# Attention scores on half of the array for every tile from 9 on, with the gate, count and logit steps moved

## The chip, the cores and the metric

The kernel runs on one core of one Trainium2 chip. The metric is the device time of one execution in microseconds. TensorE is called PE in the profile (its weight loads PEld), VectorE DVE, ScalarE ACT, GpSimd POOL, and the engine that issues most DMAs SP.

## The reference, cut to what matters

```
# attention: B=4, H=8, S=768, D=40, one decaying state per head
m_new = max(f_t + m, i_t)
C = exp(f_t + m - m_new) * C + exp(i_t - m_new) * outer(v_t, k_t)      # n likewise, with k_t
y_t = sigmoid(o_t) * (C @ q_t) / max(|n . q_t|, 1)
# x = y as (3072, 320); 8 experts, one for each token
logits = (x / (|x| + 1e-6)) @ (emb / (|emb| + 1e-6)).T / tau
e = argmax(logits);  gate = softmax(logits)[e]
x = gate * (relu(x @ w1[e]) @ w2[e])                                   # F = 1024
# dense gated layer for all tokens
out = (sigmoid(x @ w_gate) * (x @ w_val)) @ w_out                      # F = 1536
```

## The kernel before, in words

The attention runs in chunks of 128 positions. There are 6 chunks and 4 batches, so 24 tiles; tile i is chunk i // 4 of batch i % 4. The order in which each engine gets its work is written out by hand. Each engine takes its instructions in that order and waits where an operand is not ready.

For a tile, `st_S` makes the scores of 8 heads on PE (16 passes into two banks of PSUM) and calls its argument `then`, which issues other work. DVE then applies the mask twice (L463 `am`, L465 `s_ps`), ACT rounds each half to f16 (L464, L466 `ah`), POOL and DVE take the rests (L467, L471 `al`). Between L467 and L471 it calls `last`. `st_V` scales v by the input gate on POOL (`vw`), `st_V2` splits it (`vh` on ACT, `vl` on POOL). `st_AV` multiplies scores by v and state by q into `o_ps`. `post_ops` divides (`den`, x on DVE) and multiplies by the output gate (POOL, and DVE for the last four tiles). `st_XT` turns x on PE and copies it (`xt` on ACT), `st_logit` makes the logits (`l_ps`) and copies them into `rs` on DVE (L583). `st_U` makes the new state (`u_ps`, bank 5), and its `add` folds it into `cc` on DVE (L517).

In the main loop (L784), step i runs `st_AV(i)`, `st_XT(i-1)`, `post_ops(i)`, some queued side operations, `st_U(i)`, `st_S(i+3)` with `add` and `st_logit(i-1)` inside it, and `st_V(i+2)`. `st_S` uses four PSUM banks in turn, so scores of tile i+2 need the DVE to be done with those of tile i. `tp_ps` gives banks 6 and 7 in turn to all transposes, logits and counts; `o_ps` is in bank 4.

The scores can be made in two ways. k and q of an even head lie in partitions 0 to 39, those of an odd head in 64 to 103, and the other rows are zero. In the full way, each matmul takes 128 rows. In the half way (`HALF`, L718) it takes only the 40 rows of its head, so matmuls of even and odd heads use different halves of the array. Before, `HALF` holds tiles 9, 11, 13, 15, 17 and 19; tile 0 is made so as well.

`side(n)` takes n operations from the queue `sideq`. At first these are the six DVE operations of `gate_ops(2 * L, S)`, which make the gates of chunks 2 to 5 on 32 partitions x 512. Their exponentials follow at i = 5 (`st_gexp`), and `st_gates2` turns them with 8 transposes on PE. Every fourth step, `st_rank` counts on PE which place each token takes in its expert's list, and puts eight DVE operations into the queue. The running count `run` is added up on POOL. `st_order` sorts the experts by count and `st_index` builds the lists of rows.

`warm` and `fill` issue 128x512 matmuls whose result is not read. After the loop (L1388 on) the last four tiles are woven with the first expert's matmuls (`step`, L980 to L998). The rest of the kernel, experts and dense layer, is matmuls for some 600 us.

Of the kernel before, what the change touches and what calls it, by code (L numbers as in the profile page):

```python
# [22 lines left out]
def kernel(  # L23
# [46 lines left out]
    def bank(j, name):  # L70
        return psum.tile([P, 512], F32, tag=f"b{j}", name=name)
# [27 lines left out]
    ones_f = const.tile([P, P], F32, name="ones_f")  # L99
    tri_bf = const.tile([P, P], BF16, name="tri_bf")  # L100
    eofs = const.tile([P, NE], F32, name="eofs")
    run = const.tile([P, NE], BF16, name="run")
    rs = const.tile([P, NTILE, NE + 1], F32, name="rs")
    raw, ssq = rs[:, :, 0:NE], rs[:, :, NE]
    rmax = const.tile([P, NTILE], F32, name="rmax")
# [23 lines left out]
    def constants():  # L129
        nc.gpsimd.memset(ones_bf, 1.0)  # L130
        nc.gpsimd.memset(ones_f, 1.0)
        nc.gpsimd.memset(zeros, 0.0)
        nc.gpsimd.affine_select(
            out=tri_bf, in_=ones_bf, pattern=[[1, P]], compare_op=ALU.is_ge,
            fill=0.0, base=-1, channel_multiplier=-1,
        )
        ramp(eofs, [[NT, NE]], 0, 0, "eofs_i")
        ramp(run, [[NT // P, NE]], 0, 0, "run_i")
        ramp(pcol, [[0, 1]], 1, 1, "pcol_i")
        ramp(tv, [[1, NTILE]], 0, 0, "tv_i")  # L140
        ramp(iota_e, [[1, NE]], 0, 0, "iota_ei")
        ramp(blk, [[NT // P, NE], [1, GT]], 0, 0, "blk_i")
        ramp(iota_p, [[1, P]], 0, 0, "iota_i")
        for k in range(NE):
            nc.gpsimd.memset(win[:, 0, k:k + 1], float(WIN[k]))
            nc.gpsimd.memset(win[:, 1, k:k + 1], float(WIN[k] // P))
# [166 lines left out]
            out=yi, in0=yi, scalar1=-1.0, scalar2=float(0x5F3759DF), op0=ALU.mult, op1=ALU.add  # L313
        )

    def norm_steps():
        g = nc.gpsimd
        two = lambda o, x, u, w, op0, op1: g.tensor_scalar(out=o, in0=x, scalar1=u, scalar2=w, op0=op0, op1=op1)
        for _ in range(3):
            two(en_t, en_y, en_sq, en_y, ALU.mult, ALU.mult)  # L320
            two(en_t, en_t, -0.5, 1.5, ALU.mult, ALU.add)
            g.tensor_tensor(out=en_y, in0=en_t, in1=en_y, op=ALU.mult)
        g.tensor_tensor(out=en_y, in0=en_y, in1=en_sq, op=ALU.mult)
        two(en_t, en_y, 1e-6, tb, ALU.add, ALU.mult)

    def norm_scale():
        nc.vector.reciprocal(en_r, en_t)
# [66 lines left out]

    def st_gates2(lo, hi):
        n = (hi - lo) * BH
        tp = bank(5, "tp_r") if lo > 1 else tp_ps("tp_r")
        for u, src in ((0, aexp), (1, rexp)):
            for c in range(lo, hi):
                o = 256 * u + (c - lo) * BH  # L400
                nc.tensor.transpose(tp[:, o:o + BH], src[:, c * L:(c + 1) * L], ident[0:BH, 0:BH])
        for u, dst, sc in ((0, w_all, SV), (1, ri_all, SQ * SV)):
            nc.vector.tensor_scalar_mul(
                dst[:, lo:hi].rearrange("p c s -> p (c s)"), tp[:, 256 * u:256 * u + n], sc
            )
# [169 lines left out]
    def st_logit(i):  # L575
        lp = tp_ps("l_ps")
        xt = xTt.pop(i)
        for kk in range(3):
            nc.tensor.matmul(
                lp[:, 0:NE], xt[:, kk * P:(kk + 1) * P], enT[:, kk, :],  # L580
                start=(kk == 0), stop=(kk == 2),
            )
        nc.vector.tensor_copy(raw[:, i, :], lp[:, 0:NE])  # L583

    def bc(t, n):
        return t.unsqueeze(2).to_broadcast([P, B, n])
# [6 lines left out]
    def st_rank(c):  # L593
# [4 lines left out]
        for b in range(B - 1):  # L598
# [1 line left out]
                rp[:, (b + 1) * NE:], ones_bf,  # L600
                sl[:, b:b + 1, :].to_broadcast([P, B - 1 - b, NE]), start=False, stop=False,
            )
        nc.tensor.matmul(
            rp, ones_bf, run.unsqueeze(1).to_broadcast([P, B, NE]), start=False, stop=True
        )
        for b in range(B):
            nc.gpsimd.tensor_tensor(out=run, in0=run, in1=sl[:, b, :], op=ALU.add)
        pf = bp.tile([P, B, NE], F32, tag="pf", name="pf", bufs=1)
        bm = bp.tile([P, 2, B], F32, tag="bm", name="bm")
        ob = bp.tile([P, B, NB], F32, tag="ob", name="ob")  # L610
# [18 lines left out]
                out=ob, in0=blk.unsqueeze(1).to_broadcast([P, B, NB]), in1=bc(bm[:, 0], NB), op=ALU.is_equal  # L629
            ),  # L630
            lambda: v.tensor_tensor(out=oh_b[:, cs, 0], in0=ob, in1=bc(tv[:, cs], NB), op=ALU.mult),
            lambda: v.tensor_scalar_mul(oh_b[:, cs, 1], ob, pcol),
        ]

    def st_order():

        v = nc.vector
        ps = tp_ps("ord_ps")
        nc.tensor.matmul(ps[:, 0:NE], ones_bf, run, start=True, stop=True)
        key = bp.tile([P, NE], F32, tag="key", name="key", bufs=1)  # L640
        m = bp.tile([P, NE, NE], F32, tag="om", name="om", bufs=1)
        r = bp.tile([P, NE], F32, tag="or", name="or_", bufs=1)
        a = lambda t: t.unsqueeze(1).to_broadcast([P, NE, NE])
        b = lambda t: t.unsqueeze(2).to_broadcast([P, NE, NE])
        return [
            lambda: v.tensor_tensor(out=key, in0=ps[:, 0:NE], in1=eofs, op=ALU.subtract),
            lambda: v.scalar_tensor_tensor(
                out=key, in0=key, scalar=float(NE), in1=iota_e, op0=ALU.mult, op1=ALU.subtract
            ),
            lambda: v.tensor_tensor(out=m, in0=a(key), in1=b(key), op=ALU.is_gt),  # L650
            lambda: v.tensor_reduce(out=r, in_=m, axis=AX.X, op=ALU.add),
            lambda: v.tensor_tensor(out=pick, in0=a(r), in1=b(iota_e), op=ALU.is_equal),
            lambda: v.tensor_tensor(out=m, in0=pick, in1=a(iota_e), op=ALU.mult),
            lambda: v.tensor_reduce(out=key, in_=m, axis=AX.X, op=ALU.add),
            lambda: v.tensor_copy(order, key),
        ]
# [58 lines left out]
                nc.gpsimd.indirect_dma_start(xrow[n][:, u], None, src, bass.IndirectOffsetOnAxis(at, 0))  # L715

    NAHEAD = 3
    HALF = range(9, NTILE - B + 1, 2)  # L718
    sideq = []

    def side(n=1):
# [20 lines left out]


    st_V(0)
    norm_steps()
    weave(gate_ops(L, 2 * L))
    st_V2(0)
    act_zero(qk[0])
    st_gexp(L, 2 * L)
    st_S(1, None, norm_scale)  # L750
    st_V(1)
    st_V(2)
    st_S(2, lambda: (st_AV(0), st_V2(1)), lambda: first_post(0))
    load(4)
    st_U(0)
    st_V2(2)
# [3 lines left out]
    st_sig(0)  # L760
    st_sig(1)
    post[0][5]()
    st_S(3, lambda: (st_AV(1), warm(2)), lambda: first_post(1))
    st_U(1)
    st_V2(3)
    post[1][5]()
    load(5)
    sideq += gate_ops(2 * L, S)
    side(1)
    turned = []  # L770
    st_S(
        4, lambda: (turned.extend(emb_T()), st_XT(0), st_AV(2), warm(2)),
# [1 line left out]
    )  # L774
    st_sig(2)
    load_kv(6)
    post[2][5]()
    side(1)
    st_V(4)
# [2 lines left out]
    side(1)  # L782
    GX = 4
    for i in range(3, NTILE - B):  # L784
        load(i + 4)
        if i > 3:
            st_AV(i)
            warm(2 if i < 8 else i > NTILE - B - 4)
            st_XT(i - 1)
            st_V2(i + 1)  # L790
            if i == GX + 1:
                st_gexp(2 * L, S)
            post = post_ops(i)
            if i == GX + 1:
                del post[3]
            weave(post)
        else:
            warm(3)
            st_logit(0)
            st_XT(2)  # L800
            st_V2(4)
        side(1 + (i > 16))
        if i == NTILE - B - 1:
            side(len(sideq))
# [4 lines left out]
        if i == NTILE - B - 2:  # L809
            od = st_order()  # L810
            od.pop(0)()
            sideq += od
        side(1 + (i > 16))
        if i > GX:
            side(1 + (i > 16))
        if i == NTILE - B - 1:
# [17 lines left out]
        if i > B and i % B == 1:  # L834
            rk = st_rank(i // B - 1)
            rk.pop(0)()
            sideq += rk
        if i == GX + 1:
            st_gates2(2, NCH)
        if i < NTILE - B - 1:  # L840
            st_V(i + 2)
        if i == GX:
# [328 lines left out]
    def offset_ops():  # L1171
# [4 lines left out]

        def counts():
            ps[0] = tp_ps("cnt_ps")
            nc.tensor.matmul(ps[0][:, 0:NE], ones_bf, run, start=True, stop=True)

        return [
            counts,
# [976 lines left out]
```

## Time and profile before

| | |
|---|---|
| time of three runs, median (lowest to highest) | 751.93 us (751.84 to 753.35) |
| time of the profiled execution | 752.99 us |
| its span, first to last instruction | 751.2 us |
| mean granted clock of TensorE | 0.993 |
| busy: PE, DVE, ACT, POOL | 728.3, 396.0, 375.5, 398.4 us |

Busy times are sums over the span. A matmul's end is modelled, so a busy PE is not PE at its peak. Times in the rows are counted from the first instruction.

### The profile page before, as it was taken

The numbers are of one execution on the slowest core, as the hardware profiler recorded it, in microseconds if no ns is written. First come the engines' busy times: TensorE is split into PE (matmuls) and PEld (weight loads), VectorE is DVE, ScalarE is ACT, GpSimd is POOL, SyncE is SP. The second block draws the span as 40 slices with busy tenths as digits, with TensorE's granted clock in tenths as the row PEclk, the third lists the DMA queues.
The fourth block names the chain that finished last, engine by engine and source line by source line (L and its number), as shares of the span: only waits on it lengthen the run. The fifth ranks groups of instructions, "written<-read, shape, count | busy, mean of one in ns | idle before, by whom it ended". The sixth has DMA issues, their size and how long they took to land. (4 is left out here: it accounts for less than half of the span.)

```text
span 751.2 us, 17720 instructions
## 1 busy us (share of the span) xinstructions
PE 728.3 (97%) x6910; PEld 650.1 (87%) x6910; DVE 396.0 (53%) x840; ACT 375.5 (50%) x863; POOL 398.4 (53%) x464
## 2 busy tenths in 40 slices
PE   6999999999999999999999999999999999999995
PEld 5889998898888989999788888888888888888884
DVE  7878888887678877865666574131121111111111
ACT  6777766456855656665455454323333333333322
POOL 8768887547766767886142324543334424424222
PEclk9999999899999999999999999999999999999998
DMA  7746775446445556651122220000000000000001
GB/s 232 214 133 188 252 220 158 130 133 187 124 141 166 153 164 191 182 155 46 54 78 61 81 67 15 28 36 2 1 11 28 1 2 36 1 2 37 1 1 40
DMA packets 39865, 70.47 MB, mean 94 GB/s; under 512 B 4818, under 2 KB 28460, under 8 KB 39772
## 3 DMA queue, kind: packets, MB, share of 16 engines
q1 hardware_dynamic: 36764, 59.61, 26.6%
q0 software_dynamic: 3008, 9.64, 3.9%
q8 instruction: 56, 0.92, 0.5%
q14 instruction: 37, 0.30, 0.1%
HBM read 60.55 MB, written 8.68 MB: 92 GB/s over the span
## 5 line engine op out<-in xcount | busy, mean ns | idle before, releaser
L1665 POOL TENSOR_TENSOR hl<-sgm,hh 128x512 fp32r<-128x512 f32 x71 | 94.8, 1340 | 226.2 <-ACT hh L1664 226.1
L1654 DVE TENSOR_TENSOR sgm<-v_ps,sgm 128x512 f32<-128x512 f32 (+1 forms) x73 | 49.7, 682 | 228.4 <-ACT sgm L1653 228.3
L1690 PE MATMUL o_ps<-wo,hl 64*128 64x320 f32 x560 | 87.7, 307 | 0.0
L1689 PE MATMUL o_ps<-wo,hh 64*128 64x320 f32 x560 | 87.2, 305 | 0.0
L1688 PE MATMUL o_ps<-wo,hh 64*128 64x320 f32 x560 | 86.7, 304 | 0.0
L1653 ACT ACTIVATE sgm<-g_ps 128x512 f32<-128x512 f32 (+1 forms) x73 | 43.2, 593 | 77.3 <-PE g_ps L1612 77.3
L1624 ACT COPY seen<-zeros 1x1 f32<-1x1 f32 x142 | 27.0, 190 | 108.1 <-PE v_ps L1612 60.8
L1664 ACT CAST hh<-sgm 128x512 fp32r<-128x512 f32 (+1 forms) x73 | 44.8, 615 | 46.5 <-DVE sgm L1654 46.2
L1072 ACT ACTIVATE hh<-h_ps 128x256 fp32r<-128x256 f32 (+7 forms) x72 | 35.2, 489 | 56.7 <-PE h_ps L984 55.9
L1688 PEld LDWEIGHTS o_ps<-wo,hh 64*128 64x128 f32 x560 | 53.4, 185 | 6.1
L1689 PEld LDWEIGHTS o_ps<-wo,hh 64*128 64x128 f32 x560 | 53.4, 184 | 5.6
L1610 PE MATMUL v_ps<-xg,wvh 64*128 64x512 f32 x144 | 56.4, 392 | 1.5 <-ACT seen L1624 1.5
L1611 PE MATMUL v_ps<-xl,wvh 64*128 64x512 f32 x144 | 56.4, 392 | 0.0
L1611 PE MATMUL g_ps<-xl,wgh 64*128 64x512 f32 x144 | 56.4, 392 | 0.0
L1611 PE MATMUL g_ps<-xg,wgh 64*128 64x512 f32 x144 | 56.4, 392 | 0.0
L1611 PE MATMUL v_ps<-xg,wvh 64*128 64x512 f32 x144 | 56.4, 392 | 0.0
L1610 PE MATMUL g_ps<-xg,wgh 64*128 64x512 f32 x144 | 56.4, 392 | 0.0
L1610 PE MATMUL g_ps<-xh,wgh 64*128 64x512 f32 x144 | 56.3, 391 | 0.0
L1610 PE MATMUL v_ps<-xh,wvh 64*128 64x512 f32 x144 | 56.3, 391 | 0.0
L1612 PE MATMUL g_ps<-xg,wgl 64*128 64x512 f32 x144 | 56.2, 390 | 0.0
L1612 PE MATMUL v_ps<-xh,wvl 64*128 64x512 f32 x144 | 56.2, 390 | 0.0
L1612 PE MATMUL v_ps<-xg,wvl 64*128 64x512 f32 x144 | 56.2, 390 | 0.0
(360 smaller groups left out, 2615.7 us busy)
## 6 DMA issues: line engine op xcount, KB each, us to landing
kv<-in_kvo_dram SPq DMA_DIRECT2D x24, 484.0 KB
w2raw<-in_moe_w_dram SPq DMA_DIRECT2D x32, 320.0 KB
w1raw<-in_moe_w_dram SPq DMA_DIRECT2D x32, 256.0 KB
qk<-in_qkt_dram SPq DMA_DIRECT2D x48, 160.0 KB
xs<-x SPq DMA_DIRECT2D x24, 192.0 KB
w1raw<-in_moe_w_dram SPq DMA_DIRECT2D x64, 64.0 KB
raw<-in_moe_w_out_dram SPq DMA_DIRECT2D x12, 320.0 KB
raw<-in_moe_w_gate_dram SPq DMA_DIRECT2D x8, 384.0 KB
```

The costliest lines, as they stand in the source:

```text
L1072: nc.scalar.activation(out=h[f][0], in_=ps, func=AF.Relu)
L1610: lambda: nc.tensor.matmul(ps, at(wh), h[rows, kk], start=start, stop=False),
L1611: lambda: nc.tensor.matmul(ps, at(wh), l[rows, kk], start=False, stop=False),
L1612: lambda: nc.tensor.matmul(ps, at(wl), h[rows, kk], start=False, stop=stop),
L1624: passed[key] = nc.scalar.copy(seen, zeros[0:1, 0:1])
L1653: nc.scalar.activation(out=s[:, cs], in_=pg[:, cs], func=AF.Sigmoid)
L1654: nc.vector.tensor_tensor(out=s[:, cs], in0=pv[:, cs], in1=s[:, cs], op=ALU.mult)
L1664: nc.scalar.copy(gh[:, cs], s[:, cs])
L1665: e.tensor_tensor(out=gl[:, cs], in0=s[:, cs], in1=gh[:, cs], op=ALU.subtract)
L1688: lambda: nc.tensor.matmul(o, gh[rows, ts_], wh[rows], start=begin, stop=False),
L1689: lambda: nc.tensor.matmul(o, gh[rows, ts_], wl[rows], start=False, stop=False),
L1690: lambda: nc.tensor.matmul(o, gl[rows, ts_], wh[rows], start=False, stop=end),
```

## The change

- `HALF` becomes every tile from 9 to 20, so tiles 10, 12, 14, 16, 18 and 20 are made the half way too. `warm` issues one matmul more at i = 9 and 13.
- The six gate operations are queued after `st_S(1)` instead of after `load(5)`, and one is taken per tile: inside `st_S(2)`, inside `st_S(3)`, after `post[2][5]`, after `st_S(5)`, at i = 3 and at i = 4. `st_gates2(2, NCH)` moves from the end of step 5 to step 6, after `st_AV(6)` and `st_XT(5)`, and uses a bank of `tp_ps` instead of bank 5.
- The norm of the expert embeddings: one of three Newton steps runs before `st_V2(0)` and the rest after it, and `norm_scale` moves from inside `st_S(1)` to inside `st_S(2)`.
- `run` keeps four counts, one for each place in the chunk. POOL adds a chunk in one operation instead of four, and PE sums the four with four small matmuls instead of one.
- The logits of tiles 19 to 23 are copied by ACT instead of DVE, and so is L632 (`oh_b[:, cs, 1]`), an ACT activation with a scale.
- `load_qk` runs one tile further ahead.

```diff
--- before.py
+++ after.py
@@ -99,7 +99,7 @@
     ones_f = const.tile([P, P], F32, name="ones_f")
     tri_bf = const.tile([P, P], BF16, name="tri_bf")
     eofs = const.tile([P, NE], F32, name="eofs")
-    run = const.tile([P, NE], BF16, name="run")
+    run = const.tile([P, 4, NE], BF16, name="run")
     rs = const.tile([P, NTILE, NE + 1], F32, name="rs")
     raw, ssq = rs[:, :, 0:NE], rs[:, :, NE]
     rmax = const.tile([P, NTILE], F32, name="rmax")
@@ -135,7 +135,8 @@
             fill=0.0, base=-1, channel_multiplier=-1,
         )
         ramp(eofs, [[NT, NE]], 0, 0, "eofs_i")
-        ramp(run, [[NT // P, NE]], 0, 0, "run_i")
+        nc.gpsimd.memset(run[:, 1:], 0.0)
+        ramp(run[:, 0], [[NT // P, NE]], 0, 0, "run_i")
         ramp(pcol, [[0, 1]], 1, 1, "pcol_i")
         ramp(tv, [[1, NTILE]], 0, 0, "tv_i")
         ramp(iota_e, [[1, NE]], 0, 0, "iota_ei")
@@ -313,15 +314,16 @@
             out=yi, in0=yi, scalar1=-1.0, scalar2=float(0x5F3759DF), op0=ALU.mult, op1=ALU.add
         )
 
-    def norm_steps():
+    def norm_steps(n, last=False):
         g = nc.gpsimd
         two = lambda o, x, u, w, op0, op1: g.tensor_scalar(out=o, in0=x, scalar1=u, scalar2=w, op0=op0, op1=op1)
-        for _ in range(3):
+        for _ in range(n):
             two(en_t, en_y, en_sq, en_y, ALU.mult, ALU.mult)
             two(en_t, en_t, -0.5, 1.5, ALU.mult, ALU.add)
             g.tensor_tensor(out=en_y, in0=en_t, in1=en_y, op=ALU.mult)
-        g.tensor_tensor(out=en_y, in0=en_y, in1=en_sq, op=ALU.mult)
-        two(en_t, en_y, 1e-6, tb, ALU.add, ALU.mult)
+        if last:
+            g.tensor_tensor(out=en_y, in0=en_y, in1=en_sq, op=ALU.mult)
+            two(en_t, en_y, 1e-6, tb, ALU.add, ALU.mult)
 
     def norm_scale():
         nc.vector.reciprocal(en_r, en_t)
@@ -394,7 +396,7 @@
 
     def st_gates2(lo, hi):
         n = (hi - lo) * BH
-        tp = bank(5, "tp_r") if lo > 1 else tp_ps("tp_r")
+        tp = tp_ps("tp_r")
         for u, src in ((0, aexp), (1, rexp)):
             for c in range(lo, hi):
                 o = 256 * u + (c - lo) * BH
@@ -580,7 +582,7 @@
                 lp[:, 0:NE], xt[:, kk * P:(kk + 1) * P], enT[:, kk, :],
                 start=(kk == 0), stop=(kk == 2),
             )
-        nc.vector.tensor_copy(raw[:, i, :], lp[:, 0:NE])
+        (nc.vector.tensor_copy if i < NTILE - B - 1 else nc.scalar.copy)(raw[:, i, :], lp[:, 0:NE])
 
     def bc(t, n):
         return t.unsqueeze(2).to_broadcast([P, B, n])
@@ -600,11 +602,11 @@
                 rp[:, (b + 1) * NE:], ones_bf,
                 sl[:, b:b + 1, :].to_broadcast([P, B - 1 - b, NE]), start=False, stop=False,
             )
-        nc.tensor.matmul(
-            rp, ones_bf, run.unsqueeze(1).to_broadcast([P, B, NE]), start=False, stop=True
-        )
         for b in range(B):
-            nc.gpsimd.tensor_tensor(out=run, in0=run, in1=sl[:, b, :], op=ALU.add)
+            nc.tensor.matmul(
+                rp, ones_bf, run[:, b:b + 1].to_broadcast([P, B, NE]), start=False, stop=(b == B - 1)
+            )
+        nc.gpsimd.tensor_tensor(out=run, in0=run, in1=sl, op=ALU.add)
         pf = bp.tile([P, B, NE], F32, tag="pf", name="pf", bufs=1)
         bm = bp.tile([P, 2, B], F32, tag="bm", name="bm")
         ob = bp.tile([P, B, NB], F32, tag="ob", name="ob")
@@ -629,14 +631,19 @@
                 out=ob, in0=blk.unsqueeze(1).to_broadcast([P, B, NB]), in1=bc(bm[:, 0], NB), op=ALU.is_equal
             ),
             lambda: v.tensor_tensor(out=oh_b[:, cs, 0], in0=ob, in1=bc(tv[:, cs], NB), op=ALU.mult),
-            lambda: v.tensor_scalar_mul(oh_b[:, cs, 1], ob, pcol),
+            lambda: nc.scalar.activation(out=oh_b[:, cs, 1], in_=ob, func=AF.Copy, scale=pcol),
         ]
+
+    def count(ps):
+
+        for b in range(B):
+            nc.tensor.matmul(ps, ones_bf, run[:, b], start=(b == 0), stop=(b == B - 1))
 
     def st_order():
 
         v = nc.vector
         ps = tp_ps("ord_ps")
-        nc.tensor.matmul(ps[:, 0:NE], ones_bf, run, start=True, stop=True)
+        count(ps[:, 0:NE])
         key = bp.tile([P, NE], F32, tag="key", name="key", bufs=1)
         m = bp.tile([P, NE, NE], F32, tag="om", name="om", bufs=1)
         r = bp.tile([P, NE], F32, tag="or", name="or_", bufs=1)
@@ -715,7 +722,7 @@
                 nc.gpsimd.indirect_dma_start(xrow[n][:, u], None, src, bass.IndirectOffsetOnAxis(at, 0))
 
     NAHEAD = 3
-    HALF = range(9, NTILE - B + 1, 2)
+    HALF = range(9, NTILE - B + 1)
     sideq = []
 
     def side(n=1):
@@ -742,15 +749,17 @@
 
 
     st_V(0)
-    norm_steps()
+    norm_steps(1)
     weave(gate_ops(L, 2 * L))
     st_V2(0)
+    norm_steps(2, True)
     act_zero(qk[0])
     st_gexp(L, 2 * L)
-    st_S(1, None, norm_scale)
+    st_S(1)
+    sideq += gate_ops(2 * L, S)
     st_V(1)
     st_V(2)
-    st_S(2, lambda: (st_AV(0), st_V2(1)), lambda: first_post(0))
+    st_S(2, lambda: (st_AV(0), st_V2(1)), lambda: (first_post(0), norm_scale(), side(1)))
     load(4)
     st_U(0)
     st_V2(2)
@@ -760,13 +769,11 @@
     st_sig(0)
     st_sig(1)
     post[0][5]()
-    st_S(3, lambda: (st_AV(1), warm(2)), lambda: first_post(1))
+    st_S(3, lambda: (st_AV(1), warm(2)), lambda: (first_post(1), side(1)))
     st_U(1)
     st_V2(3)
     post[1][5]()
     load(5)
-    sideq += gate_ops(2 * L, S)
-    side(1)
     turned = []
     st_S(
         4, lambda: (turned.extend(emb_T()), st_XT(0), st_AV(2), warm(2)),
@@ -774,6 +781,7 @@
     )
     st_sig(2)
     load_kv(6)
+    load_qk(7)
     post[2][5]()
     side(1)
     st_V(4)
@@ -782,10 +790,12 @@
     side(1)
     GX = 4
     for i in range(3, NTILE - B):
-        load(i + 4)
+        if i + 5 < NTILE:
+            load_qk(i + 5)
+        load_kv(i + 4)
         if i > 3:
             st_AV(i)
-            warm(2 if i < 8 else i > NTILE - B - 4)
+            warm(2 if i < 8 else i % B == 1 or i > NTILE - B - 4)
             st_XT(i - 1)
             st_V2(i + 1)
             if i == GX + 1:
@@ -799,6 +809,8 @@
             st_logit(0)
             st_XT(2)
             st_V2(4)
+        if i == GX + 2:
+            st_gates2(2, NCH)
         side(1 + (i > 16))
         if i == NTILE - B - 1:
             side(len(sideq))
@@ -810,7 +822,8 @@
             od = st_order()
             od.pop(0)()
             sideq += od
-        side(1 + (i > 16))
+        if i > GX:
+            side(1 + (i > 16))
         if i > GX:
             side(1 + (i > 16))
         if i == NTILE - B - 1:
@@ -835,8 +848,6 @@
             rk = st_rank(i // B - 1)
             rk.pop(0)()
             sideq += rk
-        if i == GX + 1:
-            st_gates2(2, NCH)
         if i < NTILE - B - 1:
             st_V(i + 2)
         if i == GX:
@@ -1176,7 +1187,7 @@
 
         def counts():
             ps[0] = tp_ps("cnt_ps")
-            nc.tensor.matmul(ps[0][:, 0:NE], ones_bf, run, start=True, stop=True)
+            count(ps[0][:, 0:NE])
 
         return [
             counts,
```

## Rows read from the trace of the kernel before

**Rows 1.** Busy time of each engine (instructions), granted clock, DMA, in stretches.

```profile
core 0: us, PE busy (x) PEld busy (x) DVE busy (x) ACT busy (x) POOL busy (x), PEclk, DMA share, GB/s
50.00:75.00 25.00, 24.93 (x392) 22.73 (x388) 21.10 (x61) 18.91 (x46) 18.52 (x31) 1.00 0.51 158
...
400.00:500.00 100.00, 100.00 (x1033) 88.37 (x1032) 47.74 (x102) 43.45 (x107) 34.78 (x28) 1.00 0.15 45
```

**Rows 2.** Waits of PE from 150 us on: total, times, longest.

```profile
PE v_ps L1610 <- ACT seen L1624: 1.5, 1, 1.5
PE tp_m L970 <- DVE xl L210: 0.5, 1, 0.5
```

**Rows 3.** The same stretches view, from one tile's scores to the next's.

```profile
44.11:51.65 7.54, 6.33 (x90) 5.81 (x88) 5.27 (x19) 5.26 (x11) 4.48 (x10) 1.00 0.71 242
...
56.52:61.59 5.07, 5.07 (x76) 4.85 (x74) 4.84 (x11) 3.32 (x9) 4.12 (x7) 1.00 0.75 240
61.59:65.96 4.37, 4.37 (x76) 4.03 (x74) 3.85 (x12) 3.11 (x9) 3.28 (x5) 1.00 0.34 107
```

**Rows 4.** Timeline of PE: scores and the work after; start us, length us.

```profile
51.65 1.16 PE L451 MATMUL s_ps<-qk 40*128 40x128 f32 x16
52.74 0.83 PE L579 MATMUL l_ps<-enT,xt 128*128 128x8 f32 x6
...
56.52 2.05 PE L451 MATMUL s_ps<-qk 128*128 128x128 f32 x16
58.41 0.73 PE L579 MATMUL l_ps<-enT,xt 128*128 128x8 f32 x6
...
104.73 2.05 PE L451 MATMUL s_ps<-qk 128*128 128x128 f32 x16
```

**Rows 5.** Timeline of PE where the gates of chunks 2 to 5 are turned.

```profile
48.07 0.40 PE L401 MATMUL tp_r<-ident,it 32*128 32x32 f32 x4 [1.21 <-DVE cc L517]
...
48.65 1.12 PE L480 MATMUL o_ps<-cst,qk 128*128 128x82 f32 x8
```

**Rows 6.** Waits of DVE and POOL from 52 to 123 us.

```profile
POOL vl L435 <- ACT vh L434: 10.6, 15, 1.9
...
DVE al L471 <- ACT ah L466: 4.3, 12, 0.4
...
DVE am L463 <- PE s_ps L451: 1.7, 2, 0.9
...
DVE am L463 <- POOL vl L435: 1.0, 1, 1.0
```

**Rows 7.** Timeline of DVE: the first mask of tiles 16, 20 and 22.

```profile
87.45 0.69 DVE L463 TENSOR_TENSOR am<-s_ps,cmask 128x512 f32<-128x512 f32 x1 [0.89 <-PE s_ps L451]
...
106.67 0.69 DVE L463 TENSOR_TENSOR am<-s_ps,cmask 128x512 f32<-128x512 f32 x1 [0.98 <-POOL vl L435]
...
121.67 0.69 DVE L463 TENSOR_TENSOR am<-s_ps,cmask 128x512 f32<-128x512 f32 x1
```

**Rows 8.** Groups of DVE from 56.52 to 104.73 us: busy us, mean ns.

```profile
L632 DVE TENSOR_SCALAR oh_b<-ob,pcol 128x128 bf16<-128x128 f32 x3 | 1.4, 477 | 0.0
```

**Rows 9.** The last four tiles: waits from 123 to 152 us.

```profile
PE l_ps L579 <- DVE rs L583: 1.1, 1, 1.1
...
DVE rs L583 <- PE l_ps L579: 1.0, 1, 1.0
...
PEld tp_x L567 <- DVE x L545: 0.4, 1, 0.4
```

**Rows 10.** The stretches view, last four tiles.

```profile
140.00:150.00 10.00, 8.72 (x49) 8.21 (x49) 8.44 (x24) 3.06 (x9) 5.28 (x9) 0.66 0.59 174
```

**Rows 11.** Waits from 14 to 24 us.

```profile
DVE al L471 <- ACT ah L466: 2.4, 2, 1.2
...
PE o_ps L488 <- POOL vl L435: 1.0, 1, 1.0
```

## The prediction, made before the changed kernel ran

> **What bounds the kernel now.** I read the stretches first. From 50 to 75 us PE is busy 24.93 of 25 us, and from 400 to 500 us all the time; the granted clock is 1.00 [rows 1]. After 150 us PE waits 2.0 us in all in its two largest waits, over 600 us [rows 2]. So what makes PE arrive earlier at 150 us makes the end earlier by the same, and the change is worth what it gives in the attention.
>
> There a busy PE says little, because VectorE is as full. I cut the loop at the scores of each tile. A step that holds a full tile took 5.07 us with DVE busy 4.84; the next, with a half tile, took 4.37 us with DVE busy 3.85 [rows 3]. DVE also waits in each tile for ACT's second rounding, 4.3 us in 12 times, 0.36 each [rows 6]; that wait lies inside a tile's own chain (mask, rounding, rest) and goes with no edit here. The pair then asks DVE for 4.84 + 3.85 + 2 x 0.36 = 9.41 us, and took 9.44. From 52 to 123 us DVE's other waits of note are for PE: 1.7 us in two, and 1.0 us in one that the view puts down to POOL [rows 6]. That last one is tile 20's mask at 106.67, whose full scores began at 104.73 [rows 4, 7]: 2.05 us of scores end just there, so it was PE too. So the loop is bound by DVE and PE in turns, with almost no slack between them.
>
> **Half-array scores.** From the start of the scores to the first logit matmul, a half tile holds PE for 52.74 - 51.65 = 1.09 us and a full one for 58.41 - 56.52 = 1.89 us [rows 4]. Six tiles change, so PE gets 6 x 0.80 = 4.8 us. If PE alone set the step this would be the gain, and it is the upper end. With DVE at 9.41 of 9.44 us a pair, a quicker PE helps only where DVE waited for PE's scores: 0.89 us at tile 16 and 0.98 at tile 20 [rows 7], both full tiles that become half ones. PE is 0.8 us quicker in that very tile, and already ahead from the tiles before, so I take 1.7 us of these 1.87. At the other changed tiles PE now waits instead, at `st_U`, whose bank is free only when DVE has done `cc`. The lower end is 0, if handing over between the engines eats it.
>
> The Trainium skill has a rule against this edit: in TensorEngine Tiling (Array Packing), under PSUM Bottleneck, it says that tiling speeds up the TensorE but not the emptying of PSUM, which may become the limit. The trace agrees, with DVE's 9.41 of 9.44 us [rows 3, 6]; by the rule this edit is worth about the 1.7 us, by PE's rows alone 4.8.
>
> **L632 to ACT.** Three of them took DVE 1.4 us, 477 ns each [rows 8]; a fourth lies between there and tile 22. One operation of DVE starts before the last has ended, so I count 1.4 us for all four (between 0.8 and 1.9). DVE is the bound in that stretch, so this is a gain. ACT was busy 3.32 and 3.11 us of the two steps [rows 3] and hides it.
>
> **Gate transposes.** At the end of step 5 they wait 1.21 us for bank 5, that is for DVE's `cc`, and hold up `st_AV(6)`, which starts at 48.65 [rows 5]. That step took 7.54 us with PE busy 6.33 [rows 3]. In step 6 they come behind `st_AV(6)` and `st_XT(5)`, with a bank of `tp_ps` emptied long before. The 8 transposes stay (48.65 - 48.07 = 0.58 us), the wait goes: 1.2 us, for PE and for DVE, which here waits for both. Lower end 0.6 if a bank of `tp_ps` is late; the upper is the 1.2. Their queue is DVE's: the two copies come before the masks of tile 9, whose scores are not there yet.
>
> **Gate operations, early.** Two of the six move to where DVE waited for ACT, 2.4 us in two times [rows 11]; that frees DVE between tiles 4 and 6. But PE has work without a gap there, with its `warm` matmuls, and POOL and ACT carry the chain before. I count 0. The norm: with eight of eleven POOL operations behind `vl(0)`, PE's wait of 1.0 us goes [rows 11], but `st_AV(1)` needs POOL's `vl(1)`, and POOL has the same work before it; 0 as well. `norm_scale` now lies on ACT between tile 2's roundings and the state copies, where ACT is busy; that can cost up to 0.6. For both together -0.6 to +1.0.
>
> **Counts, loads, warm.** POOL's four additions become one and PE gets three small matmuls per chunk. Two extra `warm` matmuls cost PE about 0.2 us each, in time that PE now has over. `load_qk` goes one tile earlier on SP, ahead of `load_kv`, past no wait that blocked it before. 0 together, hidden behind DVE's chain.
>
> **Last logits on ACT.** DVE stops waiting 1.0 us for `l_ps`, PE stops waiting 1.1 us for DVE's `rs`, and the 0.4 us for the last x shrinks, because DVE comes to it earlier [rows 9]. Behind that wait the clock was low: 140 to 150 us has a mean of 0.66, which is 10 x 0.34 = 3.4 us of PE work lost [rows 10]. PE can't get all this back, because the last ranks run through DVE, busy 8.44 of those 10 us. I take 2.0 us, DVE's wait of 1.0 and two copies with L632 for the rest. Lower end 0.4 (only the wait for x), upper 4.0 (with most of the clock's loss).
>
> **Sum.** Loop 1.7 + 1.4 + 1.2 = 4.3, less 0.5 for engines that now meet with no slack (an estimate from the 0.03 us that a pair had over, between 0 and 1.7), is 3.8; with the last tiles 5.8 us. The profiled execution took 752.99, its span 751.2; less 5.8 is 747.2. The runs' median is 1.06 lower, 751.93, so I expect **746.1 us**.
>
> **Rivals.**
> - *PE was the bound.* Then six halves give 4.8, less 0.4 for the `warm` matmuls, the gates 1.2 and the tail 4.0: 9.6 us, 742.3. PE busy in the pair for all 9.44 us speaks for it [rows 3], DVE's sum against. Chance 0.12.
> - *POOL or ACT takes DVE's place in the loop.* POOL waits for ACT's `vh` 10.6 us in 15 times [rows 6], and `vh` waits for POOL's `vw`; with its 4.12 us busy in a full step [rows 3], it can hold a step at 4.5 us or more. Then the loop keeps only the gates' 1.2 us, with up to 1.5 in the tail: 749.2. Chance 0.11.
> - *Nothing measurable.* The early part loses 0.6, the gates gain 1.2 and the tail 0.4: 750.9. Chance 0.07.
> - *The clock falls in the loop: slower.* More tiles with 40-row matmuls, and a PE that waits for DVE at each, can drop it. One spell like that of 140 to 150 us costs 3.4 us [rows 10]; two eat the gain (752.9), from three on the kernel is slower, 756.3. Against it: the clock was 1.00 all through 50 to 75 us, with every other tile half [rows 1], and the fall at 143 us came behind a PE wait of 1.1 us [rows 9]; the new waits are shorter. Chance 0.14. The Trainium skill, TensorE: Matmul & The Clock Gate, under What's actually happening, says that the clock follows how busy the array has been; the spell behind the wait agrees [rows 9, 10], and by it the time would be this rival's only if the loop's waits add up.
>
> **How the numbers follow.** The forecast has 0.56. Its own range is 743.5 to 748.5, from the ends of its terms that can come together. Faster by over 0.2% (1.5 us, about what a measurement here can tell) is the forecast, the first two rivals: 0.79. Within 0.2%: 0.07. Slower: 0.14. For 8 in 10 I go from 742.5, just above the first rival's point, to 750.0, which takes in the second; the slower case, no change and a little below stay out.
>
> **What would show it.** The profile after should have the half scores in tiles 9 to 20, no wait of 1.2 us before the gate transposes and tile 9's scores about 1.2 us earlier, at 50.4. DVE's mask of tile 22, at 121.67 before [rows 7], should start at about 117.9, with PE now waiting for `cc` in `st_U`. At 150 us the shift should be near 5.8, and stay to the end. I am wrong if the clock leaves 1.00 between 50 and 125 us, if the tail's shift is smaller than the loop's, or if steps of 4.6 us and more remain with DVE waiting for POOL or ACT.

## The result, and the profile after

The changed kernel took 742.49 us in the median (742.2 to 742.75), the kernel before 751.93: a ratio of 0.987, 95% interval 0.9853 to 0.9887. The profiled execution took 742.64 us with a span of 740.6 (752.99 and 751.2 before), so the span lost 10.6 us where the prediction's sum has 5.8. The medians are 9.44 apart: the profiled execution of the kernel before was 1.06 us slower than its median, that of the changed kernel 0.15. The time is 3.6 us below the forecast of 746.1 and just under the low end of the range. The mean clock of the profiled execution rose from 0.993 to 0.997.

Where the 10.6 us came up, by five places that both traces have:

| place | before | after | shift | predicted |
|---|---|---|---|---|
| scores of tile 8 start | 44.11 | 43.56 | 0.55 | 0 |
| scores of tile 9 start | 51.65 | 49.96 | 1.69 | 1.2 |
| first mask of tile 22 | 121.67 | 114.96 | 6.71 | 3.8 |
| first copy `seen` in the dense layer | 364.0 | 355.6 | 8.4 | 5.8 |
| last copy `seen` | 736.3 | 725.7 | 10.6 | 5.8 |

The stretches view of the changed kernel, with the columns of [rows 1]: the two long stretches, the step of tile 8, two steps of the loop, and the last tiles.

```profile
50.00:75.00 25.00, 24.95 (x404) 22.83 (x404) 22.28 (x65) 20.09 (x49) 20.07 (x29) 1.00 0.60 175
400.00:500.00 100.00, 100.00 (x1036) 87.07 (x1034) 45.29 (x94) 41.56 (x102) 38.31 (x31) 1.00 0.15 46
43.56:49.96 6.40, 6.32 (x94) 5.83 (x92) 4.73 (x16) 5.98 (x14) 3.91 (x6) 1.00 0.69 233
54.72:59.10 4.38, 4.33 (x75) 4.00 (x73) 4.25 (x10) 3.00 (x8) 3.25 (x5) 1.00 0.70 215
59.10:63.40 4.30, 4.30 (x73) 3.89 (x70) 3.76 (x12) 3.98 (x12) 3.50 (x6) 1.00 0.42 144
...
140.00:150.00 10.00, 9.37 (x82) 9.06 (x80) 9.21 (x29) 5.63 (x12) 4.00 (x4) 1.00 0.52 151
```

The step that holds the gate transposes went from 7.54 to 6.40 us with the same 6.32 of PE work: the wait is gone. The pair of steps that took 5.07 and 4.37 us [rows 3] takes 4.38 and 4.30, with DVE at 4.25 + 3.76. The clock of 140 to 150 us is 1.00 (0.66 before [rows 10]); a second profile of the changed kernel, f1 below, has a spell of low clock there.

The timeline of PE in the changed kernel: the transposes, and the scores of tiles 9 and 20.

```profile
48.22 0.49 PE L569 MATMUL tp_x<-ident,x 128*128 128x128 f32 x3
48.78 0.40 PE L403 MATMUL tp_r<-ident,it 32*128 32x32 f32 x4
49.03 0.41 PE L403 MATMUL tp_r<-ident,ft 32*128 32x32 f32 x4
49.37 0.66 PE L503 MATMUL u_ps<-vw,kv 128*64 128x41 f32 x16
49.96 1.16 PE L453 MATMUL s_ps<-qk 40*128 40x128 f32 x16
...
99.73 1.16 PE L453 MATMUL s_ps<-qk 40*128 40x128 f32 x16
```

The transposes follow `st_XT(5)` without the wait of 1.21 us [rows 5]. Tile 20 has half scores and starts 5.0 us earlier than in [rows 4]. DVE's first masks of tiles 16, 20 and 22, which waited 0.89, 0.98 and 0 us before [rows 7], now wait for nothing:

```profile
82.96 0.68 DVE L465 TENSOR_TENSOR am<-s_ps,cmask 128x512 f32<-128x512 f32 x1
...
101.01 0.68 DVE L465 TENSOR_TENSOR am<-s_ps,cmask 128x512 f32<-128x512 f32 x1
...
114.96 0.68 DVE L465 TENSOR_TENSOR am<-s_ps,cmask 128x512 f32<-128x512 f32 x1
```

The waits from 51 to 118 us and, from "PE r_ps" on, from 122 to 160 us (total, times, longest):

```profile
DVE al L473 <- ACT ah L468: 4.3, 12, 0.4
DVE am L465 <- PE s_ps L453: 0.4, 2, 0.2
...
PE r_ps L599 <- DVE sel L593: 1.8, 1, 1.8
PE tp_m L981 <- DMA xrow<-xs,idx: 0.6, 1, 0.6
```

DVE's wait for ACT inside a tile is what it was [rows 6], its waits for PE fell to 0.4 us, and the wait of PE in the last tiles has another releaser (a `sel` of the last rank) and grew from 1.1 [rows 9] to 1.8 us.

### The profile page after: what moved, and what is told of

It reads as the page before. It is cut to its first block, busy times and chain, and to the rows that moved or that the text cites. A ratio compares the mean times of both kernels' runs of the same rounds, so it can differ in the third digit from the quotient of the medians.

```text
span 740.6 us, 17763 instructions
## 1 busy us (share of the span) xinstructions
PE 719.4 (97%) x6936; PEld 650.8 (88%) x6936; DVE 393.3 (53%) x829; ACT 377.7 (51%) x874; POOL 395.9 (53%) x447
## 5 line engine op out<-in xcount | busy, mean ns | idle before, releaser
L1700 PE MATMUL o_ps<-wo,hh 64*128 64x320 f32 x560 | 89.0, 304 | 0.0
L1699 PE MATMUL o_ps<-wo,hh 64*128 64x320 f32 x560 | 88.9, 304 | 0.0
L1700 PEld LDWEIGHTS o_ps<-wo,hh 64*128 64x128 f32 x560 | 55.3, 184 | 5.3
L1699 PEld LDWEIGHTS o_ps<-wo,hh 64*128 64x128 f32 x560 | 55.3, 184 | 4.1
L1084 DVE SCALAR_TENSOR_TENSOR hl<-h_ps,hh 128x256 fp32r<-128x256 f32 (+7 forms) x72 | 39.5, 550 | 32.0 <-ACT hh L1083 31.6
L1621 PE MATMUL g_ps<-xg,wgh 64*128 64x512 f32 x144 | 56.4, 392 | 0.0
L1623 PE MATMUL g_ps<-xh,wgl 64*128 64x512 f32 x144 | 56.3, 391 | 0.0
```

The costliest lines, as they stand in the source:

```text
L1084: nc.vector.scalar_tensor_tensor(out=h[f][1], in0=ps, scalar=0.0, in1=h[f][0], op0=ALU.max, op1=ALU.subtract)
L1621: lambda: nc.tensor.matmul(ps, at(wh), h[rows, kk], start=start, stop=False),
L1623: lambda: nc.tensor.matmul(ps, at(wl), h[rows, kk], start=False, stop=stop),
L1699: lambda: nc.tensor.matmul(o, gh[rows, ts_], wh[rows], start=begin, stop=False),
L1700: lambda: nc.tensor.matmul(o, gh[rows, ts_], wl[rows], start=False, stop=False),
```

## The experiments

Each ratio is to the kernel before on the same chip in the same session. "Loop" is the time from the first mask of tile 10 to that of tile 22 in the profiled run, "dense" that between the first and last `seen`, and the last column is where, between 20 and 126 us, the granted clock fell from 1.00 to about 0.50 (1.2 GHz), called a spell below. Loop, dense and spells come from one profile of each run. In the cuts of the edits `...` stands for lines left out.

| run | ratio [95%] | loop | dense | clock low at |
|---|---|---|---|---|
| before (first chip) | | 62.76 | 372.3 | |
| changed (first chip) | 0.987 [0.9853, 0.9887] | 58.31 | 370.1 | |
| e1_half_only | 0.9999 [0.9977, 1.0021] | 62.81 | 373.3 | 49-53, 79-84 |
| e2_ohb_only | 0.9988 [0.9968, 1.0008] | 61.60 | 373.4 | 49-53 |
| e3_gates_only | 0.9959 [0.9944, 0.9974] | 63.27 | 373.3 | |
| e4_logits_only | 0.9994 [0.9979, 1.0009] | 62.75 | 373.3 | 50-55 |
| f1_after_again | 0.9873 [0.9857, 0.989] | 58.87 | 371.8 | 51-55 |
| f2_less_half | 0.9927 [0.991, 0.9943] | 62.37 | 371.7 | |
| f3_one_count | 0.9924 [0.9908, 0.9941] | 60.32 | 373.6 | |
| f4_ohb_on_vector | 0.9894 [0.9878, 0.9911] | 60.37 | 371.7 | |
| g1_run_size | 0.9976 [0.9959, 0.9993] | 62.70 | 371.3 | 48-55 |
| g2_pe_more | 0.992 [0.9898, 0.9941] | 61.89 | 371.3 | |
| g3_dve_more | 1.0004 [0.9981, 1.0026] | 68.82 | 371.3 | 77-88, 104-108 |
| g4_loop_trio | 0.9916 [0.9897, 0.9935] | 58.37 | 371.4 | 48-55 |
| h1_one_count_64 | 0.9915 [0.9885, 0.9944] | 60.40 | 371.3 | |
| h2_half_ohb_64 | 0.9935 [0.9919, 0.9952] | 61.71 | 371.4 | 48-52, 79-83 |
| h3_count_only | 0.9994 [0.9981, 1.0007] | 63.32 | 370.6 | 48-56 |
| h4_half_more | 0.9909 [0.9874, 0.9943] | 61.43 | 371.3 | 51-65 |
| p1_run_32 | 1.0001 [0.9981, 1.0021] | 62.70 | 372.3 | 49-54 |
| p2_run_80 | 1.0018 [0.9998, 1.0038] | 63.18 | 373.0 | 36-40, 50-54 |

**One part alone, in the kernel before.** e1_half_only takes the new half scores with their `warm` matmuls:

```diff
-    HALF = range(9, NTILE - B + 1, 2)
+    HALF = range(9, NTILE - B + 1)
...
-            warm(2 if i < 8 else i > NTILE - B - 4)
+            warm(2 if i < 8 else i % B == 1 or i > NTILE - B - 4)
```

> The kernel before, with only the half scores for tiles 9 to 20 and the two extra warm matmuls. Theory V (VectorE sets the step, as predicted): only the two waits of its mask for PE's scores go (0.89 and 0.98 us), so about 1.7 us faster, near 750.2. Theory P (PE sets the step): six halves of 0.80 less 0.4 for the warm matmuls, 4.4 us faster, near 747.5. The granted clock stays 1.00 from 50 to 125 us by both.

No gain shows. The interval leaves out Theory P's 4.4 us and just reaches Theory V's 1.7. Against both theories a spell came in the middle of the loop and took a part: outside it, the loop is shorter by 0.1 us from the mask of tile 10 to that of tile 14 (19.32 against 19.45) and by 0.4 from tile 16 to 22 (33.85 against 34.22).

e2_ohb_only moves L632 to ACT:

```diff
-            lambda: v.tensor_scalar_mul(oh_b[:, cs, 1], ob, pcol),
+            lambda: nc.scalar.activation(out=oh_b[:, cs, 1], in_=ob, func=AF.Copy, scale=pcol),
```

> The kernel before, with only the product with pcol (L632) on ScalarE. Theory V: VectorE loses four operations of its chain, 1.2 to 1.4 us faster, near 750.6. Theory P: no change, 751.9.

The loop is 1.16 us shorter, near the 1.4 of its term; the time's interval includes no change.

e3_gates_only has the gate operations one per tile and the transposes in step 6, without the edits to the norm:

```diff
-        tp = bank(5, "tp_r") if lo > 1 else tp_ps("tp_r")
+        tp = tp_ps("tp_r")
...
+    sideq += gate_ops(2 * L, S)
...
+        if i == GX + 2:
+            st_gates2(2, NCH)
...
-        if i == GX + 1:
-            st_gates2(2, NCH)
```

> The kernel before, with only the early gate operations one per tile and the eight transposes moved to step 6. Predicted 1.2 us faster (750.7), the wait of 1.21 us for bank 5 gone. If the early operations count as well, tile 9's scores start 1.7 us earlier as in the changed kernel (49.96 against 51.65), near 750.2.

It is the only part that is faster by itself by more than its interval. It is also the only one of the four with no low clock near 50 us. All nine of these kernels that keep the transposes at their old place, behind PE's wait of 1.1 to 1.2 us, have such a spell there; the profile of before hasn't. So e3's 2.5 us (751.68 against 754.20 in the medians) may hold the loss of a spell besides the 1.2 us.

e4_logits_only:

```diff
-        nc.vector.tensor_copy(raw[:, i, :], lp[:, 0:NE])
+        (nc.vector.tensor_copy if i < NTILE - B - 1 else nc.scalar.copy)(raw[:, i, :], lp[:, 0:NE])
```

> The kernel before, with only the last five logit copies on ScalarE. Predicted 2.0 us faster (749.9). If the low clock from 143 to 149 us came from PE's wait for VectorE's copy, it goes and up to 3.4 us come back (748.5); if the last ranks on VectorE hold all, 0.4 to 1 us.

The 2.0 us forecast did not come; the interval, from 1.6 us of gain to 0.7 of loss, leaves it out. PE's wait for `rs` is gone and the clock stays at 1.00 in the last tiles, but PE now waits there for two other operations of DVE (118 to 157 us):

```profile
PE r_ps L597 <- DVE sel L591: 1.9, 1, 1.9
PE ix_ps L663 <- DVE oh_b L632: 1.4, 1, 1.4
```

The four ratios multiply to 0.994, less than half of the change: something is missing, or the parts need each other.

**One part taken out of the changed kernel.** f1_after_again is the changed kernel on the chip of the three that follow.

> The changed kernel unaltered, as a base for the other three on the same chip. First mask of tile 10 to that of tile 22: 58.3 us as in its first profile (62.8 before). Granted clock 1.00 from 20 to 150 us.

The ratio is that of the first chip and the loop is 58.87 us, but the clock did not stay at 1.00: it fell at 51 us and again at 140 us, behind the wait of 1.8 us for `sel` that the first profile has too.

f2_less_half takes the two edits of e1 out again.

```diff
-    HALF = range(9, NTILE - B + 1)
+    HALF = range(9, NTILE - B + 1, 2)
...
```

> The changed kernel with the half scores of tiles 9, 11, ..., 19 alone and without the two extra warm matmuls. Theory V (VectorE sets the step): the two waits for PE's scores come back, 1.7 us slower than the changed kernel, 60.0 us from mask 10 to mask 22. Theory B (both bound: PE's time is worth its price once VectorE has been relieved): 3 to 4.4 us slower, 61.5 or more.

The half scores, which showed no gain alone, are worth 4.0 us here (749.82 less 745.84), as Theory B has it.

f3_one_count has a single running count again:

```diff
-    run = const.tile([P, 4, NE], BF16, name="run")
+    run = const.tile([P, NE], BF16, name="run")
...
-        nc.gpsimd.tensor_tensor(out=run, in0=run, in1=sl, op=ALU.add)
+        for b in range(B):
+            nc.gpsimd.tensor_tensor(out=run, in0=run, in1=sl[:, b, :], op=ALU.add)
```

> The changed kernel with one running count, added up by GpSimd in four operations, as before. Theory G (GpSimd's chain from the rest to the next v is what held VectorE's small operations): 1 to 2 us slower, most of it in the steps with ranks (masks 9 to 10, 13 to 14, 17 to 18). Theory V: within 0.3 us.

The part that the prediction priced at nothing costs 3.7 us when it is taken out: some 1.5 in the loop and 1.8 in the dense layer, where it does no work.

f4_ohb_on_vector takes out the edit of e2:

```diff
-            lambda: nc.scalar.activation(out=oh_b[:, cs, 1], in_=ob, func=AF.Copy, scale=pcol),
+            lambda: v.tensor_scalar_mul(oh_b[:, cs, 1], ob, pcol),
```

> The changed kernel with the product with pcol (L632) back on VectorE. Theory V: 1.2 us slower from mask 10 to 22, and the last ranks later by 0.3. If the shorter small operations of VectorE came with this edit (0.43 to 0.19 us each), 2 us and more slower.

1.7 us (747.56 less 745.84), near its term of 1.4.

**The dense layer: place or work?** g1_run_size, in the kernel before, only makes the tile of the count larger; no instruction differs but in addresses.

```diff
-    run = const.tile([P, NE], BF16, name="run")
+    run4 = const.tile([P, 4, NE], BF16, name="run")
+    run = run4[:, 0]
```

> The kernel before, in which only the tile of the running count is four times as large (64 instead of 16 bytes in each partition, three quarters unused), so that tiles behind it lie 48 bytes further. Theory A (the dense layer's pace depends on where its operands lie): from the first to the last reading of the dense layer's results on ScalarE 371.7 us instead of 373.3, and 1.7 us faster in all. Theory N (chance): no change, within 0.5 us.

The kernel is 1.8 us faster (752.45 against 754.21), and the dense layer 1 to 2 us quicker. Its first and last copy, in g1 and then in the kernel before:

```profile
L1625 ACT COPY seen<-zeros x142: 174/190/193, 364.4 to 735.7; 1x1 f32<-1x1 f32 x142
```

```profile
L1624 ACT COPY seen<-zeros x142: 186/190/193, 364.0 to 736.3; 1x1 f32<-1x1 f32 x142
```

735.7 - 364.4 = 371.3 us against 372.3 in this profile and 373.3 in e1 to e4. Two more sizes, which put everything behind the tile 16 and 64 bytes further instead of 48 (p1_run_32, shown, and p2_run_80 with 5 in place of 2):

```diff
-    run = const.tile([P, NE], BF16, name="run")
+    run4 = const.tile([P, 2, NE], BF16, name="run")
+    run = run4[:, 0]
```

> The kernel before with the tile of counts at 32 bytes per partition instead of 16, so that everything behind it lies 16 bytes further. Theory A (the place within 64 bytes decides, and the 48 bytes of the change end on a good one): the dense layer between its first and last copy takes 372.3 to 373.4 us as before, or a value between. Theory B (any place but the old one is quicker): 371.3 us and ratio 0.998, as with 48 bytes.

> The same with 80 bytes, so that everything lies 64 bytes further. Theory A (the place within 64 bytes decides): as before, 372.3 to 373.4 us and ratio 1.000. Theory B (any other place): 371.3 us and 0.998.

372.3 and 373.0: no gain. Every kernel with 48 bytes took 370.1 to 371.8, every other 372.3 to 373.6, on one chip too (f1, f2 and f4 371.7 to 371.8, f3 373.6). So the place decides, and 48 bytes is a better one than 0, 16 or 64. It shows in the matmuls themselves, of which this is one group of many, from 370 to 720 us (busy us, mean ns): the kernel before, then g1.

```profile
L1690 PE MATMUL o_ps<-wo,hl 64*128 64x320 f32 x530 | 83.1, 307 | 0.0
```

```profile
L1691 PE MATMUL o_ps<-wo,hl 64*128 64x320 f32 x532 | 81.8, 302 | 0.0
```

**Which engine bounds the changed loop?** g2_pe_more gives PE two `warm` matmuls more in each step from 8 to 19, g3_dve_more gives DVE a copy of 128x128 there.

```diff
-            warm(2 if i < 8 else i % B == 1 or i > NTILE - B - 4)
+            warm(2 if i < 8 else 2 + (i % B == 1 or i > NTILE - B - 4))
```

> The changed kernel with two warm matmuls more in each step from 8 to 19, 12 x 0.43 = 5.2 us of TensorE. Theory P (TensorE sets the step): 4.5 to 5.2 us slower. Theory V (VectorE sets it): under 1.5 us. Theory B (both are at their limit): 3 to 5 us.

```diff
+            if i >= 8:
+                nc.vector.tensor_copy(iota_p, iota_p)
```

> The changed kernel with one VectorE copy more (iota_p onto itself, 128x128) in each step from 8 to 19, some 12 x 0.2 = 2.4 us of VectorE. Theory V: 2.0 to 2.5 us slower. Theory P: under 0.5. Theory B: 1.5 to 2.5.

By f1's ratio the changed kernel would take 0.9873 x 754.21 = 744.6 us on this chip. More PE work costs 3.9 us, as Theory B has it. DVE's twelve copies were priced at 2.4 us, were busy for 5.6 in the trace and cost 9.5, more than any of the theories. So both engines are at their limit. What DVE's delay costs beyond itself came with two spells; no run parts the one from the other. g3's stretches:

```profile
56.00:77.00 21.00, 19.71 (x315) 17.98 (x315) 19.03 (x51) 14.38 (x37) 16.44 (x24) 1.00 0.66 193
77.00:88.00 11.00, 10.26 (x120) 9.09 (x118) 9.30 (x25) 5.88 (x15) 6.36 (x9) 0.53 0.71 217
...
104.00:108.00 4.00, 3.87 (x48) 3.38 (x48) 3.58 (x11) 2.18 (x6) 3.28 (x5) 0.57 0.64 165
```

PE was busy 19.71 of 21 us, and then the clock was at 0.53 for 11 us.

**Counts, half scores and L632 together.** g4_loop_trio puts these three parts into the kernel before (edits of e1 and e2, those of f3 turned round).

```diff
+    run = const.tile([P, 4, NE], BF16, name="run")
...
+        nc.gpsimd.tensor_tensor(out=run, in0=run, in1=sl, op=ALU.add)
...
+    HALF = range(9, NTILE - B + 1)
...
+            lambda: nc.scalar.activation(out=oh_b[:, cs, 1], in_=ob, func=AF.Copy, scale=pcol),
```

> The kernel before with the three edits of the loop together: half scores, L632 on ScalarE, four counts. Alone, the first gave nothing clear and the second 1.3 us. Theory B (each engine's relief pays only beside the others'): first mask of tile 10 to that of tile 22 in 58.5 to 59.5 us instead of 62.8, and 5 us or more faster in all with the dense layer's 1.7. If they only add: 3 us.

It is 5.7 us faster (748.55 against 754.21), and its loop is 58.37 us, that of the changed kernel; half scores and L632 alone gave 0 and 1.16. h1_one_count_64 is f3 with the tile kept at 64 bytes, h2_half_ohb_64 is g4 less the four counts, at 64 bytes too, and h3_count_only has only the four counts. The count in h1 and h2:

```diff
+    run4 = const.tile([P, 4, NE], BF16, name="run")
+    run = run4[:, 0]
...
+        for b in range(B):
+            nc.gpsimd.tensor_tensor(out=run, in0=run, in1=sl[:, b, :], op=ALU.add)
```

> The changed kernel with one running count and four GpSimd additions per chunk, but in a tile of 64 bytes per partition, so that the addresses behind it stay. Theory A (the additions on GpSimd stretch DVE's small operations of the rank steps): the first masks of tiles 10 and 22 lie 60 us or more apart (58.3 in the changed kernel), the means of L615 and L623 return from about 185 to over 350 ns, the dense layer keeps 371 to 372 us between its first and last copy, ratio to before about 0.990. Theory B (only the place counts): masks at 58.3 to 58.9 apart and ratio 0.987.

> The kernel before with half scores on tiles 9 to 20, L632 on ScalarE, and the counts as before in a tile of 64 bytes. It is the run with these two and four counts (0.9916) less the four counts. Theory A (counts matter in the loop once PE is quicker): tiles 10 to 22 over about 60 us instead of 58.4, ratio about 0.994. Theory B (half scores and L632 are enough): 58.4 and 0.992.

The edit of h3:

```diff
+    run = const.tile([P, 4, NE], BF16, name="run")
...
+        nc.gpsimd.tensor_tensor(out=run, in0=run, in1=sl, op=ALU.add)
```

> The kernel before with four counts alone. Theory A: the small DVE operations shorten, but every second step waits for PE's full scores, so tiles 10 to 22 take 62 us or a little less (62.76 before); the dense layer takes 371.4 instead of 373.3; ratio 0.997, as with the larger tile alone. Theory B (the additions are worth as much by themselves as in the changed kernel): 61 us or less, ratio 0.994.

With the place held, one count makes the loop 60.40 us, 2.1 more than in the changed kernel (1.5 more than in f1), with the clock at 1.00 in both. By the time alone h1's interval still overlaps f1's. Without the faster PE the four counts give nothing (63.32): h3 missed its forecast of 0.997, although its dense layer took 370.6. h2 has 61.71, 3.3 more than with four counts; h1 has the same three parts in the loop and no spell, so 1.3 of it is likely the spell's at 79 us. So the counts are worth some 2 us, but only beside the half scores. Where they go is in the loop as a whole, h1 and then the changed kernel (columns of [rows 1]):

```profile
56.47:116.87 60.40, 58.32 (x926) 52.93 (x926) 52.58 (x155) 44.28 (x113) 49.64 (x77) 1.00 0.65 200
```

```profile
56.65:114.96 58.31, 58.16 (x948) 53.36 (x949) 50.95 (x155) 44.62 (x113) 48.28 (x68) 1.00 0.69 205
```

With the same 155 instructions DVE is busy 1.6 us longer in h1. Two of its smallest operations hold that, again h1 and then the changed kernel (busy us, mean ns; 56 to 118 us). The expectation had named L623 and L615; L615 is L617 here and stayed at 171 ns in h1.

```profile
L623 DVE SCALAR_TENSOR_TENSOR bm<-bm,posf 128x4 f32<-128x4 f32 x3 | 1.6, 538 | 0.0
L620 DVE TENSOR_SCALAR bm<-bm 128x4 f32<-128x4 f32 x3 | 1.1, 378 | 0.1
```

```profile
L623 DVE SCALAR_TENSOR_TENSOR bm<-bm,posf 128x4 f32<-128x4 f32 x3 | 0.6, 191 | 0.0
L620 DVE TENSOR_SCALAR bm<-bm 128x4 f32<-128x4 f32 x3 | 0.5, 170 | 0.1
```

Most of the rest is a wait that the changed kernel doesn't have: the matmul of `st_order` waits for GpSimd's last addition, and DVE for that matmul (h1, 56 to 117 us).

```profile
PE ord_ps L639 <- POOL run L609: 0.8, 1, 0.8
DVE key L652 <- PE ord_ps L639: 0.4, 1, 0.4
```

Why the operations stretch is in the timelines (start, length): first h1, then the changed kernel, in the same step.

```profile
73.15 0.73 DVE L623 SCALAR_TENSOR_TENSOR bm<-bm,posf 128x4 f32<-128x4 f32 x1
...
73.12 0.74 POOL L427 TENSOR_TENSOR vw<-kv,w_all 128x328 f32<-128x328 f32 x1
```

```profile
73.23 0.15 DVE L623 SCALAR_TENSOR_TENSOR bm<-bm,posf 128x4 f32<-128x4 f32 x1
...
72.50 0.73 POOL L427 TENSOR_TENSOR vw<-kv,w_all 128x328 f32<-128x328 f32 x1
```

The same DVE operation on 128x4 elements took 0.73 us when it began beside GpSimd's `vw`, and ended with it (73.88 and 73.86); with `vw` at its end it took 0.15. The kernel before has the same:

```profile
76.23 0.53 DVE L621 SCALAR_TENSOR_TENSOR bm<-bm,posf 128x4 f32<-128x4 f32 x1
...
76.01 0.74 POOL L425 TENSOR_TENSOR vw<-kv,w_all 128x328 f32<-128x328 f32 x1
```

They end at 76.76 and 76.75. Four additions take GpSimd 1.03 us per rank in this trace, the one 0.24 in the changed kernel, so `vw` comes earlier and leaves these operations of DVE alone.

h4_half_more makes all tiles from 1 on with half scores:

```diff
-    HALF = range(9, NTILE - B + 1)
+    HALF = range(1, NTILE)
```

> The changed kernel with half scores for all tiles from 1 on, also the last three. Theory A (where DVE and the chain of POOL and ACT set the steps, quicker scores give nothing): ratio 0.986 to 0.988, as the changed kernel. Theory B (PE is a limit before tile 9 too): 2 us less, 0.984. Against both: a PE that waits in tiles 4 to 8 loses its clock, and the time rises.

It is not faster than the changed kernel; its interval is too wide for more. Its stretches:

```profile
40.00:51.00 11.00, 10.22 (x166) 9.08 (x167) 9.06 (x29) 10.28 (x21) 7.80 (x12) 1.00 0.66 201
...
52.00:64.00 12.00, 12.00 (x118) 10.57 (x119) 7.09 (x22) 5.12 (x14) 6.16 (x9) 0.50 0.48 145
```

PE was busy 10.22 of 11 us (10.92 in the changed kernel), waited 0.8 us once for DVE, and then ran 12 us at 0.50; from tile 12 on its steps are those of the changed kernel.

## Why the prediction was wrong

Right in sign, wrong in size: 10.6 us of span, 9.44 in the medians, where the sum has 5.8. In the pair of profiles the difference by its terms is 0.5 before tile 9, 2.4 in the loop, -0.3 in the last tiles and 2.2 in the dense layer. The reading that DVE and PE bound the loop in turns held; the prices did not follow it, for they took each edit by itself against DVE as it was found.

- **Gate transposes, 1.2: right in the profile.** The step lost 1.14 us; the medians of e3 lost 2.5, of which a spell may be a part. **Gate operations, early, 0:** 0.55 us by tile 8, inside its -0.6 to +1.0.
- **L632, 1.4: right**, 1.7 in f4. **Half-array scores, 1.7: mis-sized.** The waits at tiles 16 and 20 are gone, but a price per edit holds only in one order. The half scores showed no gain alone and were worth 4.0 us in the changed kernel. The loop as a whole, in the kernel before, in e1 and in f2:

```profile
58.91:121.67 62.76, 62.23 (x953) 57.93 (x952) 54.02 (x158) 43.30 (x109) 49.95 (x77) 1.00 0.64 197
```

```profile
59.91:122.72 62.81, 61.20 (x950) 55.42 (x948) 54.59 (x158) 43.24 (x109) 49.70 (x77) 0.97 0.64 197
```

```profile
56.51:118.88 62.37, 62.31 (x970) 58.47 (x968) 51.99 (x154) 43.89 (x113) 48.68 (x68) 1.00 0.64 193
```

PE was full before the change too, 62.23 of 62.76 us. Made quicker alone (e1), it idles for 1.6 us, and DVE waits for scores only once, for 1.0 us at the end of its spell. With DVE relieved alone (f2), PE is busy all the time, and DVE waits 3.5 us for scores. With both, PE is busy 58.16 of 58.31 us, so PE's waits for `cc`, which the prediction gave as a sign, did not come. I weighed the rule of the Trainium skill (TensorEngine Tiling (Array Packing), PSUM Bottleneck) for this one edit alone; e1 agrees with it, and two other edits relieved DVE.
- **"Counts ... 0 together, hidden behind DVE's chain", and "less 0.5 for engines that now meet with no slack": the step that failed.** From the first mask of tile 9 to that of tile 22 the loop lost 5.0 us instead of 2.6. No loss in handing over appeared, and the counts brought 1.5 to 2.1 (f1 and the first profile, against h1). The four additions weren't hidden behind DVE's chain; they lengthened it, in h1 by 1.6 us of longer operations and a wait of 0.4. My sum of 4.84 + 3.85 us for DVE already held stretched operations: in that pair L621 took 0.34 us, and L632 0.87 where it took 0.28 in the next three ranks. The sign was in the trace of before, in the groups of DVE from 56 to 125 us (busy us, mean ns), two operations on 128x4 elements each:

```profile
L621 DVE SCALAR_TENSOR_TENSOR bm<-bm,posf 128x4 f32<-128x4 f32 x4 | 1.4, 362 | 0.0
...
L618 DVE TENSOR_SCALAR bm<-bm 128x4 f32<-128x4 f32 x3 | 0.5, 170 | 0.1
```

The Trainium skill, SBUF — State Buffer, under SBUF: two separate sides, says that DVE and GpSimd share a pair of ports as an exclusive lock, which whichever starts first holds for its whole instruction, also when the DVE operation has two SBUF inputs and the GpSimd one reads SBUF. The pairs of equal ends agree, and I did not weigh it.

- **Dense layer, no term: missing.** 2.2 us in the pair of profiles, from 48 bytes; in a time by itself it shows in g1 (0.9976) and not in h3 (0.9994, with a spell and a loop 0.6 us longer).
- **Last logits, 2.0: not borne out.** Alone (e4) they gave 0.5 us, with 2.0 outside the interval, because waits for `sel` and L632 came in place of the one for `rs`. That the table has 1.7 us there (8.4 less 6.71) is luck: from the first mask of tile 22 to the first `seen` it is 242.3 us before and 240.6 in the first profile, but 242.3 in f1 and f2, whose last tiles have the same edits. At the first index matmul the shift was 9.8 us (150.64 to 140.88), with the clock's loss given back; 1.4 of it was lost again by 364 us. The new waits of 0.6 us for a gather and 1.8 for `sel` are near it; no run separates them. In f1 the clock fell behind that wait for `sel`:

```profile
140.00:144.00 4.00, 4.00 (x31) 3.91 (x28) 2.63 (x11) 1.49 (x4) 1.27 (x3) 0.57 0.37 107
```

- **Rivals.** "PE was the bound" names 742.3 us, and that the time is so near is luck: a quicker PE alone gave nothing (e1), and more work for DVE costs too (g3, f4). "The clock falls in the loop" did not come in the first profile of the changed kernel; in f1 the clock left 1.00 at 51 to 55 us. That a spell can come in the loop is shown by e1, h2, g3 and h4, each behind a stretch in which PE was not busy all the time (22.42 of 23 us in e1); but f3 had 22.32 of 23 us and no spell. POOL does set DVE's pace, but the change relieved it rather than running into it.

Open: how e3's 2.5 us divide between the wait and the spell (f1 has a spell at 51 us without that wait), and how the clock's spells enter the medians. An exact split of the loop's 5.0 us among three edits doesn't exist apart from an order.

## What to carry to other kernels

Where two engines take turns as the bound, price edits to them together: one alone gives little, the second then seems to give all. Before a busy time is used as an engine's need, look for operations whose duration doesn't fit their size, and for what runs beside them on GpSimd. And when a tile changes its size, everything behind it moves: compare the pace of loops that the edit doesn't touch.

## What was not expected of the hardware

- The same dense layer, with the same instructions, took 370.1 to 371.8 us where the tiles lie 48 bytes further, and 372.3 to 373.6 with 0, 16 or 64. Why is open.
- The granted clock doesn't follow from one wait. Behind PE's wait of 1.1 to 1.2 us near 48 us it fell to 0.50 (1.2 GHz) in nine kernels and stayed at 1.00 in the profile of before; in f1 it fell there without such a wait; behind the changed kernel's 1.8 us in the last tiles it stayed at 1.00 in one profile and fell to 0.50 in another (f1).
